# Attention scores on four row groups with four PSUM banks per unit, a new order of attention work, and weight preparation in pieces

## The chip, the core and the metric

The kernel runs on one core of a Trainium2 chip. The metric is device time in microseconds (us) of one execution. PE is the matrix engine, ACT the scalar engine (it does the exponentials), DVE the vector engine, POOL the GpSimd engine, SP the engine that issues most transfers. All engines work from static instruction lists, which are filled by a small list scheduler in the kernel's own source. It gives each operation an estimated duration and a priority (a lower number goes first), and fixes the order on every engine before anything runs. An edit to a priority, a bank or an engine therefore makes a new plan for all engines.

Times of one kernel mostly agree within 1%. Some runs are "slow" (over 1.5% above the fastest of the same kernel) and are kept out of comparisons. The ratios below are the mean time of one kernel's fast runs over that of the other's fast runs of the same rounds, so not quite the ratio of the medians that are quoted.

## The reference

A transformer block with two halves. The sequence has 2048 rows of width 448. The first half is attention with 16 heads of 28, in a sliding window of 256. The second is a gated MLP which also mixes along the sequence with a 2048 x 2048 matrix. Cut to what matters:

```python
h = layernorm(x) * (1 + ca) + sa
q, k, v = split(h @ wqkv)                        # 16 heads of 28
scores = einsum('bhqd,bhkd->bhqk', q, k) * 28**-0.5
p = softmax(where(0 <= q_idx - k_idx < 256, scores, -1e9))
x = x + ga * (einsum('bhqk,bhkd->bhqd', p, v) @ wo)
h = layernorm(x) * (1 + cb) + sb
z1, z2 = split(gelu(h @ w_in)); z2 = layernorm(z2)
x = x + gb * ((z1 * (w_sp @ z2 + b_sp)) @ w_out)
```

## The kernel before

The queries are worked in 16 blocks of 128 rows (`j`). Each block needs the scores against at most three key blocks (`kb`). Q and K are stored transposed and padded to 32 rows a head, four heads on top of each other, so a score matmul has a contraction of 32 and uses one of the array's four row groups. A score unit is 8 matmuls on two row groups, written to a pair of PSUM banks; one exp instruction on ACT then reads the whole pair.

```python
B_S = bank((0, 1), (2, 3))            # pairs for scores
B_MISC = bank((4,), (5,), (6,), (7,)) # PV, wo, projections, bias rows, gates
...
for hx in range(2):                              # half of the heads
    for bi, kb in enumerate(kbs):
        pr = j + (hx * nb + bi) / (2.0 * nb)     # priority of the unit
        ten = Ten(B_S)
        def s_fn(e, ...):
            for g in range(4):
                for i in range(2):
                    r = 2 * hx + i               # row group
                    last = mm(e, ps[:, ten.slot + i, g * 128:(g + 1) * 128],
                              QKT[32*r:32*r+32, 4+g, kb*128:(kb+1)*128],
                              QKT[32*r:32*r+32, g, j*128:(j+1)*128], True, True, tile_position=(32*r, 0))
        # exp on ACT, causal / window mask on POOL
    # PV of this half of the heads, priority j + 0.5 + 0.5 * hx + 0.1
# reciprocal and normalisation (DVE), transpose (DMA), wo (PE), residual x1, layernorm 2
```

The layernorm of the input (`xn`) runs on DVE. The second half's weights are prepared during attention: four bias rows (PE and a DVE cast), four products on `w_in`, and one product over all of `w_out` (`woutg`), which reads a gate from PSUM.

The softmax here doesn't subtract the row's maximum and nothing guards it: scores larger than these inputs give would overflow.

## Time and profile before

| | before |
|---|---|
| median of three runs | 331.76 us |
| first exp to last exp | 22.4 to 154.8 us |
| first MLP matmul to the end | 154.3 to 329.3 us: 175.1 us |
| TensorE clock at half speed after 20 us | 47.8 us |

The first lines to look at are the page's busy times and its rows of 40 slices (8.2 us a slice; a digit is tenths of the slice; PEclk is the granted TensorE clock).

```profile
PE 306.5 (93%) x2675; PEld 159.9 (49%) x2686; DVE 182.3 (55%) x405; ACT 131.9 (40%) x164; POOL 94.1 (29%) x110
...
PE   6697899799979999799999999999999999999995
...
ACT  3277167694666768898355666200000000000000
...
PEclk9789699999975589965899999999999999999999
```

There are two stages. From slice 19 on PE is full, from slice 20 on at full clock; that is the MLP. Before it PE has gaps, and besides short dips up to slice 4 the clock row has two long valleys, slices 11 to 14 and 17 to 19.

The first valley by stretches of 5 us. The columns are each engine's busy us with its number of instructions (PE, PEld, DVE, ACT, POOL), the mean granted clock, DMA share and GB/s.

```profile
90.00:95.00 5.00, 3.06 (x60) 2.19 (x60) 2.60 (x6) 2.86 (x4) 4.62 (x3) 0.91 0.64 124
95.00:100.00 5.00, 5.00 (x64) 3.05 (x60) 3.56 (x9) 3.86 (x4) 2.72 (x3) 0.50 0.16 37
100.00:105.00 5.00, 5.00 (x58) 2.70 (x54) 0.76 (x2) 3.07 (x3) 2.85 (x3) 0.50 0.49 88
105.00:110.00 5.00, 5.00 (x67) 3.09 (x66) 3.71 (x9) 3.49 (x4) 2.77 (x4) 0.50 0.32 66
110.00:115.00 5.00, 5.00 (x56) 2.46 (x55) 0.42 (x1) 3.50 (x4) 2.55 (x3) 0.50 0.45 89
```

PE idles for some 2 us of 90 to 95, and then the clock is half for 24 us. In those 24 us PE works more slowly: the `wo` matmuls start every 373 ns, against 189 at full clock, and the projections of 256 columns every 213, against 109 (medians of this trace).

The groups of instructions by shape (busy us, mean ns of one, then the idle time of the engine just before them and what ended it):

```profile
L625 ACT ACTIVATE PT<-ps 128x1024 bf16<-128x1024 f32 x90 | 88.1, 1026 | 39.5 <-PE ps L412 39.4
L412 PE MATMUL ps<-QKT 32*128 32x128 bf16 x720 | 38.2, 241 | 6.4 <-ACT PT L625 6.4
L490 DVE TENSOR_SCALAR xn<-x_sb,mv_all,rs_all 128x448 bf16<-128x448 bf16 x16 | 8.2, 545 | 1.0 <-POOL rs_all L465 0.9
```

ACT idles 39.5 us before its exps, and PE ended that idling. So PE is what holds attention up. A PE mean of 241 ns here is a latency, not a cost, because matmuls overlap: the eight of the unit below end 0.40 us after the first starts. The cost is read from the timeline as start to next start: the 8 matmuls of a unit, then the next kind.

```profile
122.19 0.40 PE L412 MATMUL ps<-QKT 32*128 32x128 bf16 x8
122.51 0.72 PE L412 MATMUL ps<-hT,WQK 112*128 112x256 bf16 x5
```

From 122.19 to 122.51 is the unit's cost. Over all warm units it is 0.328 us in the median, and 0.54 us at half clock.

### The profile page before, as it was taken

To read this page: it belongs to the slowest core of one execution; us is meant where nothing else is said; L and a number is where in the kernel's file an instruction comes from. 1 tells how busy PE (TensorE), PEld (TensorE's weight loads), DVE (VectorE), ACT (ScalarE), POOL (GpSimd) and SP (SyncE) were. 2 spreads that over 40 slices of the span, in tenths; PEclk is the share of its full clock that TensorE was granted. 3 is DMA by queue.
4 is the path that set the end of the run, shared out by engine and by line. 5 is a ranking of instruction groups with operands and counts; after the bars stand their busy time and mean duration, and the time that the engine had idled before them with its cause. 6 is when DMAs were issued, how large, how long until landed. Compare 5 with 4: busy or idle time off the path is not lost.

```text
span 329.3 us, 6418 instructions
## 1 busy us (share of the span) xinstructions
PE 306.5 (93%) x2675; PEld 159.9 (49%) x2686; DVE 182.3 (55%) x405; ACT 131.9 (40%) x164; POOL 94.1 (29%) x110
## 2 busy tenths in 40 slices
PE   6697899799979999799999999999999999999995
PEld 2464355364556466564444444444444444444442
DVE  5579898898853377644588772132243242324232
ACT  3277167694666768898355666200000000000000
POOL 4025336484474556776123121000000000000000
PEclk9789699999975589965899999999999999999999
DMA  7933794712335317575779900000010010001001
GB/s 188 275 105 66 156 192 126 192 36 50 65 66 99 66 34 114 90 114 115 147 133 218 180 2 0 0 2 0 0 58 0 0 39 19 0 2 56 0 0 56
DMA packets 67195, 25.18 MB, mean 76 GB/s; under 512 B 58464, under 2 KB 66592, under 8 KB 67168
## 3 DMA queue, kind: packets, MB, share of 16 engines
q1 hardware_dynamic: 67040, 24.79, 35.8%
q8 instruction: 21, 0.34, 0.5%
q14 instruction: 6, 0.05, 0.1%
q10 hardware_dynamic: 128, 0.00, 0.0%
HBM read 8.78 MB, written 1.84 MB: 32 GB/s over the span
## 4 chain that ended last, share of the span: by engine, by line
PE 79%; DVE 9%; DMA 5%; ACT 3%; issue 1%; POOL 1%; SPq 1%; DVEq 0%
PE ps L412 79%; ACT PT L625 3%; DMA x_sb<-in_A_x_dram 3%; DVE hT L529 3%; DVE xn L490 2%; DVE st_all L469 1%; DMA hT<-xn 1%; DMA oT<-o_sb 1%; DVE QKT L566 1%; POOL PT L633 1%; DVE wo_sb L458 1%; DVE hT L518 1%; DVE fin L839 0%; SPq L358 0%; DVE o_sb L657 0%
## 5 line engine op out<-in xcount | busy, mean ns | idle before, releaser
L625 ACT ACTIVATE PT<-ps 128x1024 bf16<-128x1024 f32 x90 | 88.1, 1026 | 39.5 <-PE ps L412 39.4
L633 POOL TENSOR_SCALAR_AFFINE_SELECT PT<-PT 128x1024 bf16<-128x1024 bf16 x60 | 68.8, 1157 | 39.8 <-ACT PT L625 39.5
L412 PE MATMUL ps<-w_spA,z 128*128 128x512 bf16 x327 | 76.3, 379 | 0.5
L817 DVE TENSOR_TENSOR tmpg<-ps,bsp_bc 128x512 bf16<-128x512 f32 x28 | 19.4, 692 | 74.5 <-PE ps L412 74.5
L412 PEld LDWEIGHTS ps<-w_spA,z 128*128 128x128 bf16 x336 | 32.9, 98 | 39.4
L412 PE MATMUL ps<-QKT 32*128 32x128 bf16 x720 | 38.2, 241 | 6.4 <-ACT PT L625 6.4
L412 PE MATMUL ps<-hT,WQK 112*128 112x256 bf16 (+1 forms) x192 | 42.4, 357 | 1.9 <-DVE hT L529 1.6
L465 POOL TENSOR_TENSOR rs_all<-ve_all,neghalf 128x1 f32<-128x1 f32 (+2 forms) x39 | 23.0, 597 | 65.2 <-DVE ve_all L463 65.0
L412 PEld LDWEIGHTS ps<-QKT 32*128 32x128 bf16 x720 | 23.0, 102 | 25.7 <-PE ps L412 19.9
L412 PE MATMUL ps<-w_spB,z 128*128 128x512 bf16 x110 | 28.5, 379 | 0.1
L412 PE MATMUL ps<-w_in_sb,hT 112*128 112x448 bf16 (+1 forms) x128 | 28.4, 366 | 0.0
L412 PE MATMUL ps<-hT,w_in_sb 112*128 112x512 bf16 x112 | 27.7, 387 | 0.0
L673 DVE TENSOR_TENSOR x_sb<-ps,x_sb 128x448 bf16<-128x448 f32 x16 | 9.9, 622 | 28.2 <-PE ps L412 28.2
L412 PEld LDWEIGHTS ps<-hT,WQK 112*128 112x128 bf16 x192 | 18.3, 109 | 14.9 <-DVE hT L529 3.6
L412 PEld LDWEIGHTS ps<-Vaug,PT 128*128 128x128 bf16 x720 | 22.1, 99 | 6.9 <-DVE QKT L566 1.8
L412 PE MATMUL ps<-Vaug,PT 128*128 128x29 bf16 x720 | 23.5, 179 | 1.3 <-POOL PT L633 1.3
L796 ACT ACTIVATE z1T<-ps 128x512 bf16<-128x512 f32 x28 | 16.7, 597 | 17.9 <-PE ps L412 17.9
L412 PE MATMUL ps<-w_out_sb,z1T 128*128 128x448 bf16 x112 | 21.8, 352 | 0.0
L566 DVE CAST QKT<-ps 128x256 bf16<-128x256 f32 (+1 forms) x33 | 17.7, 544 | 7.0 <-PE ps L412 6.7
L469 DVE BATCH_NORM_STATS2 st_all<-z2raw 128x6 f32<-128x448 bf16 x32 | 18.4, 607 | 3.4 <-ACT z2raw L776 3.4
L412 PE MATMUL ps<-wo_sb,oT 112*128 112x448 bf16 x64 | 18.1, 413 | 2.4 <-DVE QKT L566 2.0
L469 DVE BATCH_NORM_STATS2 st_all<-x_sb 128x6 f32<-128x448 bf16 x32 | 19.1, 606 | 1.8 <-DMA x_sb<-in_A_x_dram 1.5
(57 smaller groups left out, 239.9 us busy)
## 6 DMA issues: line engine op xcount, KB each, us to landing
out_dram<-fin SPq DMA_DIRECT2D x16, 112.0 KB, 1.7
wmod_sb<-in_w_mod_dram SPq DMA_DIRECT2D x2, 784.0 KB, 6.5
w_in_sb<-in_B_w_in_dram SPq DMA_DIRECT2D x4, 392.0 KB, 4.2
x_sb<-in_A_x_dram SPq DMA_DIRECT2D x3, 448.0 KB, 10.1
wqk_raw<-in_A_wqkv_dram SPq DMA_DIRECT2D x2, 392.0 KB, 8.3
wmod_sb<-in_w_mod_dram SPq DMA_DIRECT2D x2, 392.0 KB, 7.7
bsp_bc<-in_B_b_sp_dram SPq DMA_DIRECT2D x1, 512.0 KB, 4.6
x_sb<-in_A_x_dram SPq DMA_DIRECT2D x2, 224.0 KB, 5.9
```

The source lines that it names most:

```text
L412: return e.matmul(out_, lhsT=lhsT, rhs=rhs, start=st, stop=sp, **kw)
L458: t_wog = P.op("wog1", -1.1, [("dve", dve_ns(4 * D), lambda e: e.tensor_tensor(wo_sb[0:KP, :, :], wo_sb[0:KP, :, :], ps[0:KP, ten_g1.slot, ...
L465: return P.op(name + "rs", prio, [("pool", 515 + 150 * (t1 - t0 - 1), lambda e: e.tensor_tensor(rs_all[:, slot, t0:t1], ve_all[:, slot, t0 ...
L469: st = [P.op("%sst%d" % (name, i), prio, [("dve", dve_ns(D, base=65), lambda e, i=i, s_=s_: e.bn_stats(st_all[:, slot, t, i, :], s_()))], ...
L490: xn_op[t] = P.op("xn%d" % t, pr + 0.1, [("dve", 310, lambda e, t=t, ten=ten: e.tensor_scalar(xn[:, ten.slot, :, 0:KP], x_sb[:, t, :].rear ...
L529: hT_op[b].append(P.op("hT%d_%d" % (b, cc), pr + 0.1, [("dve", 190 + 0.27 * 128 * n, lambda e, cc=cc: e.tensor_scalar(hT[0:KP, cc, t0 * 12 ...
L566: return e.tensor_copy(QKT[:, g, t0 * 128:t1 * 128], ps[:, ten.slot, 0:n])
L625: return e.activation(PT[:, pt.slot, :, :], ps[:, ten.slot:ten.slot + 2, :], ACT.Exp, scale=SCALE)
L633: return e.affine_select(out=v, in_=v, pattern=[[0, 8], [s_, 128]], compare_op=ALU.is_ge if diag else ALU.is_gt, fill=0.0, base=0, channel ...
L673: x1_op[j] = P.op("x1_%d" % j, pr, [("dve", 545, lambda e, j=j, wt=wt: e.tensor_tensor(x_sb[:, j, :], ps[:, wt.slot, 0:D], x_sb[:, j, :], ...
L796: z1_op[(ft, tb)] = P.op("z1g%d_%d" % (tb, ft), pr, [("act", act_ns(512), lambda e, tb=tb, ft=ft, ten=ten: e.activation(z1T[:, ft, tb * 51 ...
L817: a = P.op("ga%d_%d" % (tb, ft), pr, [("dve", 610, lambda e, tb=tb, ten=ten, tg=tg: e.tensor_tensor(tmpg[:, tg.slot, :], ps[:, ten.slot, : ...
```

## The change

Its intent: use all four row groups at once, so that one unit of 16 matmuls does what two units of 8 did, in about the time of one. A unit then writes two bank pairs. To let the next unit start while ACT still reads the last one, there is a third pair, which leaves two single banks for everything else. The weight preparation is cut into pieces and moved to the end of attention. The diff also changes the order of work: scores get a priority four query blocks ahead (`j - 4`) and PV nearly three ahead (`j - 2.95`). Twelve of the sixteen `xn` go to POOL. Cut to its core:

```diff
-    B_S = bank((0, 1), (2, 3))
-    B_MISC = bank((4,), (5,), (6,), (7,))
+    B_S = bank((0, 1), (2, 3), (4, 5))
+    B_MISC = bank((6,), (7,))
@@
-        for hx in range(2):
-            for bi, kb in enumerate(kbs):
-                pr = j + (hx * nb + bi) / (2.0 * nb)
-                ten = Ten(B_S)
+        for bi, kb in enumerate(kbs):
+            pr = j - 4 + bi / float(nb)
+            tens = [Ten(B_S), Ten(B_S)]
@@
-                        for i in range(2):
-                            r = 2 * hx + i
-                            last = mm(e, ps[:, ten.slot + i, ...
+                    for r in range(4):
+                        last = mm(e, ps[:, tens[r // 2].slot + r % 2, ...
@@
-            pv = P.op("PV%d_%d" % (j, hx), j + 0.5 + 0.5 * hx + 0.1, ...
+            pv = P.op("PV%d_%d" % (j, hx), j - 2.95 + 0.01 * hx, ...
@@
-                xn_op[t] = P.op(..., [("dve", 310, ...
+                xn_op[t] = P.op(..., [("dve", 310, xn_fn)] if b < NPE else [("pool", 600, xn_fn)], ...
@@  bias rows from priority 6.3 to 10.5 and later, w_in products from 7.5 to 12.5 and later,
@@  both also held back to set score units (33 and on, 40 and on, of 45)
-    t_woutg = P.op("woutg", 9.3, one product over 7 x 448 from PSUM)
+    t_gb = P.op("gbcp", 13.3, copy of the gate to SBUF)
+    t_woutg = [P.op("woutg%d" % k, 150 + k, product over 448) for k in range(7)]
```

Cut away: the scheduler's support for an operation that takes two tensors of banks, the scaling of `wo` in four pieces, projections of the first blocks allowed in all banks, and new points in the list of score units from which later projections and weight loads may start.

More of the change, by code (lines that the diff above doesn't have):

```diff
@@ L66, in op @@
         self.ops.append(o)
-        if alloc is not None:
-            alloc(o)
+        for t in flat(alloc):
+            t(o)
         for t in flat(uses):
@@ L71, in op, with slot_time @@
         return o
-    def slot_time(self, ten):
+    def slot_time(self, ten, taken=()):
         best = None
@@ L77, in slot_time @@
             for r in opt:
+                if r in taken:
+                    tm = None
+                    break
                 prev = self.last.get(r)
@@ L105, in schedule @@
                 if o.alloc is not None:
-                    st = self.slot_time(o.alloc)
-                    if st is None:
+                    st, taken = [], []
+                    for ten in flat(o.alloc):
+                        got = self.slot_time(ten, taken)
+                        if got is None:
+                            break
+                        st.append((ten, got[1]))
+                        taken += got[1]
+                        dep_t = max(dep_t, got[0])
+                    if len(st) < len(list(flat(o.alloc))):
                         continue
-                    dep_t = max(dep_t, st[0])
                 best = None
@@ L126, in schedule @@
             if o.alloc is not None:
-                for r in st[1]:
-                    prev = self.last.get(r)
-                    if prev is not None:
-                        o.extra.extend(prev.users)
-                    self.last[r] = o.alloc
-                o.alloc.got = st[1]
+                for ten, slots in st:
+                    for r in slots:
+                        prev = self.last.get(r)
+                        if prev is not None:
+                            o.extra.extend(prev.users)
+                        self.last[r] = ten
+                    ten.got = slots
             o.eng, o.fn, o.start, o.end = eng, fn, est, fin
@@ L211, in run @@
                 fn(e).then_inc(self.sems[key], inc)
+REL = {2: (1, 8), 3: (8, 19), 4: (19, 28), 5: (28, 37)}
+MISC = (12, 33, 2, 40, 1, 33, 18, 4)
 def mm_ns(n):
@@ L251, in bass_adaLN_cond__sliding_block__mixer_gmlp__prompt_kernel @@
     SCALE = float(DH) ** -0.5
-    ARENA = 207 * 1024
+    ARENA = 207 * 1024 + 512
     arena = nc.alloc_sbuf_tensor("arena", [128, ARENA // 2], BF16)
@@ L285, in bass_adaLN_cond__sliding_block__mixer_gmlp__prompt_kernel @@
     neghalf, _, _ = alloc("neghalf", [128, NT], F32)
+    gb_sb, _, _ = alloc("gb_sb", [128, D], F32)
     w_spA, wspA_off, wspA_end = alloc("w_spA", [128, 12, S], BF16)
@@ L457, in bass_adaLN_cond__sliding_block__mixer_gmlp__prompt_kernel @@
     g1, ten_g1 = gate("gateA", -1.2, 2, t_wmG)
-    t_wog = P.op("wog1", -1.1, [("dve", dve_ns(4 * D), lambda e: e.tensor_tensor(
-        wo_sb[0:KP, :, :], wo_sb[0:KP, :, :], ps[0:KP, ten_g1.slot, 0:D].unsqueeze(1).broadcast_to([KP, KC, D]), ALU.mult))],
-        [g1, t_wo], uses=[ten_g1])
+    t_wog = [P.op("wog%d" % k, -1.1, [("dve", dve_ns(D), lambda e, k=k: e.tensor_tensor(
+        wo_sb[0:KP, k, :], wo_sb[0:KP, k, :], ps[0:KP, ten_g1.slot, 0:D], ALU.mult))], [g1, t_wo], uses=[ten_g1]) for k in range(KC)]
     def ln_rs(name, prio, slot, t0, t1, deps):
@@ L489, in ln1, with xn_fn @@
                 xn_ten[t] = ten
-                xn_op[t] = P.op("xn%d" % t, pr + 0.1, [("dve", 310, lambda e, t=t, ten=ten: e.tensor_scalar(
-                    xn[:, ten.slot, :, 0:KP], x_sb[:, t, :].rearrange("p (k d) -> p k d", d=KP), mv_all[:, 0, t, 0:1], rs_all[:, 0, t:t + 1],
-                    ALU.subtract, ALU.mult))], [rs, t_xpad], alloc=ten)
+                def xn_fn(e, t=t, ten=ten):
+                    return e.tensor_scalar(xn[:, ten.slot, :, 0:KP], x_sb[:, t, :].rearrange("p (k d) -> p k d", d=KP),
+                                           mv_all[:, 0, t, 0:1], rs_all[:, 0, t:t + 1], ALU.subtract, ALU.mult)
+                xn_op[t] = P.op("xn%d" % t, pr + 0.1, [("dve", 310, xn_fn)] if b < NPE else [("pool", 600, xn_fn)], [rs, t_xpad], alloc=ten)
     hT_op, xnT = {}, {}
@@ L502, in transp @@
             for cc in range(KC):
-                ten = Ten(B_MISC)
+                ten = Ten(B_ALL)
                 mms = []
@@ L528, in transp, with md_fn @@
             for cc in range(KC):
-                hT_op[b].append(P.op("hT%d_%d" % (b, cc), pr + 0.1, [("dve", 190 + 0.27 * 128 * n, lambda e, cc=cc: e.tensor_scalar(
-                    hT[0:KP, cc, t0 * 128:t1 * 128], hT[0:KP, cc, t0 * 128:t1 * 128],
-                    modT[0:KP, 4 + cc:5 + cc], modT[0:KP, cc:cc + 1], ALU.mult, ALU.add))], xnT[b] + t_modA))
+                def md_fn(e, cc=cc):
+                    return e.tensor_scalar(hT[0:KP, cc, t0 * 128:t1 * 128], hT[0:KP, cc, t0 * 128:t1 * 128],
+                                           modT[0:KP, 4 + cc:5 + cc], modT[0:KP, cc:cc + 1], ALU.mult, ALU.add)
+                hT_op[b].append(P.op("hT%d_%d" % (b, cc), pr + 0.1, [("dve", 190 + 0.27 * 128 * n, md_fn)], xnT[b] + t_modA))
     t_wqkc = []
@@ L550, in qkv @@
         for k, g in enumerate((0, 4, 1, 5, 2, 6, 3, 7)):
-            ten = Ten(B_MISC)
+            ten = Ten(B_ALL if b < 2 else B_MISC)
             m = []
@@ L571, in qkv @@
         for t in range(t0, t1):
-            ten = Ten(B_MISC)
+            ten = Ten(B_ALL if b < 2 else B_MISC)
             m = []
@@ L603, in bass_adaLN_cond__sliding_block__mixer_gmlp__prompt_kernel, with s_fn @@
         pvs = []
-        for hx in range(2):
-            halves = []
-            for bi, kb in enumerate(kbs):
-                pr = j + (hx * nb + bi) / (2.0 * nb)
-                ten = Ten(B_S)
-                def s_fn(e, j=j, kb=kb, hx=hx, ten=ten):
-                    last = None
-                    for g in range(4):
-                        for i in range(2):
-                            r = 2 * hx + i
-                            last = mm(e, ps[:, ten.slot + i, g * 128:(g + 1) * 128],
-                                      QKT[32 * r:32 * r + 32, 4 + g, kb * 128:(kb + 1) * 128],
-                                      QKT[32 * r:32 * r + 32, g, j * 128:(j + 1) * 128], True, True, tile_position=(32 * r, 0))
-                    return last
-                deps = [QK_op[(g, blk_of[j])] for g in range(4)] + [QK_op[(4 + g, blk_of[kb])] for g in range(4)]
-                s_op = P.op("S%d_%d_%d" % (j, hx, bi), pr, [("pe", 410, s_fn)], deps, alloc=ten)
-                all_S.append(s_op)
+        halves = {0: [], 1: []}
+        for bi, kb in enumerate(kbs):
+            pr = j - 4 + bi / float(nb)
+            tens = [Ten(B_S), Ten(B_S)]
+            def s_fn(e, j=j, kb=kb, tens=tens):
+                last = None
+                for g in range(4):
+                    for r in range(4):
+                        last = mm(e, ps[:, tens[r // 2].slot + r % 2, g * 128:(g + 1) * 128],
+                                  QKT[32 * r:32 * r + 32, 4 + g, kb * 128:(kb + 1) * 128],
+                                  QKT[32 * r:32 * r + 32, g, j * 128:(j + 1) * 128], True, True, tile_position=(32 * r, 0))
+                return last
+            deps = [QK_op[(g, blk_of[j])] for g in range(4)] + [QK_op[(4 + g, blk_of[kb])] for g in range(4)]
+            s_op = P.op("S%d_%d" % (j, bi), pr, [("pe", 410, s_fn)], deps, alloc=tens)
+            all_S.append(s_op)
+            for hx in range(2):
+                ten = tens[hx]
                 pt = Ten(rot("pt", NPT))
@@ L635, in bass_adaLN_cond__sliding_block__mixer_gmlp__prompt_kernel, with pv_fn @@
                     done = P.op("M%d_%d_%d" % (j, hx, bi), pr, [("pool", pool_ns(1024), m_pool)], [e_op], uses=[pt])
-                halves.append((kb, pt, done))
-            def pv_fn(e, hx=hx, halves=halves, nb=nb, pv_ten=pv_ten):
+                halves[hx].append((kb, pt, done))
+        for hx in range(2):
+            def pv_fn(e, hx=hx, halves=halves[hx], nb=nb, pv_ten=pv_ten):
                 last = None
@@ L646, in pv_fn @@
                 return last
-            pv = P.op("PV%d_%d" % (j, hx), j + 0.5 + 0.5 * hx + 0.1, [("pe", 8 * nb * 25.5, pv_fn)],
-                      [d for _, _, d in halves] + [V_op[kb] for kb in kbs],
-                      alloc=pv_ten if hx == 0 else None, uses=[pt for _, pt, _ in halves] + ([pv_ten] if hx else []), order=pvs[:1])
+            pv = P.op("PV%d_%d" % (j, hx), j - 2.95 + 0.01 * hx, [("pe", 8 * nb * 25.5, pv_fn)],
+                      [d for _, _, d in halves[hx]] + [V_op[kb] for kb in kbs],
+                      alloc=pv_ten if hx == 0 else None, uses=[pt for _, pt, _ in halves[hx]] + ([pv_ten] if hx else []), order=pvs[:1])
             pvs.append(pv)
@@ L669, in wo_fn @@
                 return mm(e, ps[:, wt.slot, 0:D], oT[0:KP, oTt.slot, kc, :], wo_sb[0:KP, kc, :], kc == 0, kc == KC - 1)
-            wos.append(P.op("wo%d_%d" % (j, kc), pr, [("pe", mm_ns(D), wo_fn)], [t1, t_wog], alloc=None if kc else wt,
+            wos.append(P.op("wo%d_%d" % (j, kc), pr, [("pe", mm_ns(D), wo_fn)], [t1] + t_wog, alloc=None if kc else wt,
                             uses=[oTt] + ([wt] if kc else []), order=wos[-1:]))
@@ L689, in bass_adaLN_cond__sliding_block__mixer_gmlp__prompt_kernel @@
         first_S[j] = i
-        i += 2 * min(j + 1, 3)
+        i += min(j + 1, 3)
     def release(ops, s0, s1):
@@ L695, in release @@
             o.order.append(all_S[max(0, min(NS - 1, k))])
-    release(chains[2], 2, first_S[4] - 2)
-    release(chains[3], first_S[4] - 2, first_S[8] - 3)
-    release(chains[4], first_S[8] - 3, first_S[12] - 9)
-    release(chains[5], first_S[12] - 9, first_S[14] - 3)
+    for b_, (s0, s1) in REL.items():
+        release(chains[b_], s0, s1)
     m2, ten_m2 = mod_cols("modB", 6.0, (3, 4), t_wmB)
@@ L714, in fn @@
             return last
-        b = P.op("bz%d" % q, 6.3 + 0.3 * q, [("pe", 4 * mm_ns(D), fn)], [t_sbT] + t_win, alloc=ten)
+        b = P.op("bz%d" % q, 10.5 + 0.5 * q, [("pe", 4 * mm_ns(D), fn)], [t_sbT] + t_win, alloc=ten)
         bias_mm.append(b)
-        bias_ev.append(P.op("bze%d" % q, 6.4 + 0.3 * q, [("dve", dve_ns(D), lambda e, q=q, ten=ten: e.tensor_copy(
+        bias_ev.append(P.op("bze%d" % q, 10.6 + 0.5 * q, [("dve", dve_ns(D), lambda e, q=q, ten=ten: e.tensor_copy(
             bias_row[0:1, q * D:(q + 1) * D], ps[0:1, ten.slot, 0:D]))], [b] + t_wqkc, uses=[ten]))
-    t_brow = P.op("brow", 7.5, [("sp", 400, lambda e: e.dma_start(w_in_sb[KP:KP + 1, 3, :], bias_row[0:1, :]))], bias_ev,
+    t_brow = P.op("brow", 12.5, [("sp", 400, lambda e: e.dma_start(w_in_sb[KP:KP + 1, 3, :], bias_row[0:1, :]))], bias_ev,
                   table="load", dma=(3584, 2500, 165.0))
@@ L722, in bass_adaLN_cond__sliding_block__mixer_gmlp__prompt_kernel @@
     for kc in range(KC):
-        t_wing.append(P.op("wing%d" % kc, 7.5 + kc * 0.5, [("dve", 670, lambda e, kc=kc: e.tensor_scalar(
+        t_wing.append(P.op("wing%d" % kc, 12.5 + kc * 0.5, [("dve", 670, lambda e, kc=kc: e.tensor_scalar(
             w_in_sb[0:KP, kc, :], w_in_sb[0:KP, kc, :], modT[0:KP, 12 + kc:13 + kc], None, ALU.mult))], bias_mm + t_modB))
-    g2, ten_g2 = gate("gateB", 9.2, 5, t_wmB)
-    t_woutg = P.op("woutg", 9.3, [("dve", dve_ns(7 * D), lambda e: e.tensor_tensor(
-        w_out_sb[:], w_out_sb[:], ps[:, ten_g2.slot, 0:D].unsqueeze(1).broadcast_to([128, 7, D]), ALU.mult))], [g2] + t_wout, uses=[ten_g2])
+    g2, ten_g2 = gate("gateB", 13.2, 5, t_wmB)
+    t_gb = P.op("gbcp", 13.3, [("dve", dve_ns(D), lambda e: e.tensor_copy(gb_sb[:], ps[:, ten_g2.slot, 0:D]))], [g2], uses=[ten_g2])
+    t_woutg = [P.op("woutg%d" % k, 150 + k, [("dve", dve_ns(D), lambda e, k=k: e.tensor_tensor(
+        w_out_sb[:, k, :], w_out_sb[:, k, :], gb_sb[:], ALU.mult))], [t_gb] + t_wout) for k in range(7)]
     for n, o in enumerate(t_wmB + t_win + t_wout):
         o.order.append(xnT[2][-1])
-        o.order.append(all_S[min(NS - 1, 6 + 2 * n)])
-    m2.order.append(all_S[first_S[5]])
+        o.order.append(all_S[min(NS - 1, 3 + n)])
+    m2.order.append(all_S[MISC[0]])
+    for q in range(4):
+        bias_mm[q].order.append(all_S[MISC[1] + MISC[2] * q])
+        t_wing[1 + q].order.append(all_S[MISC[3] + MISC[4] * q])
+    g2.order.append(all_S[MISC[5]])
     mod_done = [m1, m2, g1, g2]
@@ L749, in bass_adaLN_cond__sliding_block__mixer_gmlp__prompt_kernel @@
             if hf == 0:
-                o.order.append(all_S[min(NS - 1, first_S[7] + 4 * n)])
+                o.order.append(all_S[min(NS - 1, MISC[6] + MISC[7] * n // 2)])
             else:
@@ L835, in bass_adaLN_cond__sliding_block__mixer_gmlp__prompt_kernel @@
                 parts.append(P.op("out%d_%d" % (t, lo), pr + i * 0.01 + (0.1 if lo else 0), [("pe", (hi - lo) * mm_ns(D), fn)],
-                                  [u_op[(ft, tb)] for ft in range(lo, hi)] + [t_woutg], alloc=ten if lo == 0 else None,
+                                  [u_op[(ft, tb)] for ft in range(lo, hi)] + t_woutg, alloc=ten if lo == 0 else None,
                                   uses=[ten] if lo else [], order=parts[:1]))
```

## The prediction

> **What bounds it now.** The page gives PE 93% busy, DVE 55%, ACT 40%. By stretches of the trace there are two stages. From about 154 us to the end (329) PE is gap-free at clock 1.0: the gated-MLP stage, some 175 us, which the change hardly touches (seven short `w_out` products on a DVE with slack there). Before it lies attention, 20 to 154 us: 134 us, in which the timeline's start-to-start times give PE 122 us of issue and 12 us of idle. The 90 exps on ACT (1.03 us each, about 0.93 in a row) need only some 84 us, but run from 22 to 154: 1.47 us each. So PE, not ACT, paces attention, with DVE close behind between 25 and 80 us (18 of 20 us busy).
>
> **Cost of scores.** A score unit of 8 matmuls (two row groups) takes 0.33 us of PE warm: pairs step every 56 ns, 0.22 us, plus about 0.10 us before the next kind's weights load. At clock 0.5 it is 0.54 us. The 90 units cost 34 us.[...]
>
> **Removed.** 45 units of 16 matmuls on four row groups remain. If quartets step every 56 ns, a unit still takes 0.33 us; if each weight load needs its 25 to 28 ns (the spacing of the PV matmuls), 0.50. I expect 0.38: about 13 us of PE saved[...].
> Twelve `xn` (0.55 us on DVE) go to POOL. The four of the first big block end at 28 us, held up by the 2.0 us `wo` product; on POOL they would end near 23. The exps' gap of 33 to 43 us, which waits for that block, shrinks: 4 us.
> The 3.4 us `w_out` product and the bias preparation leave mid-attention.
>
> **Added.** Score pairs take six PSUM banks; PV, `wo`, projections and bias share two instead of four. By my estimate per query block: PV holds a bank 3.3 us (less than now: both halves come together), `wo` 2, three projections 2 each: 11 us on two banks, 5.5 us, about ACT's 5.7 for six exps. New PE waits for DVE evictions: +4 us.
>
> **Clock.** The page's clock row and the stretches show 0.5 from 94 to 118 and 142 to 159 us, each after a few us of PE idling. I estimate 15 us lost to it in attention (`wo` matmul 387 against 208 ns). A denser PE should lose less, but as ACT comes nearer to bounding, idling returns late in attention: −4 us.
>
> **Sum.** −13 −4 −4 +4 = −17, and −1 for preparation moved into idle time: 331.8 − 18 = about 314 us, range 300 to 327. Chances: faster 0.82, same 0.13, slower 0.05.
>
> **What would show it.** The last exp at about 136 us instead of 154, 1.2 to 1.3 us per exp; the dense stage still 174 to 176 us; a warm 16-matmul unit at 0.33 to 0.50 us; PE waits on the QKT, Vaug and x_sb evictions up from about 5 us to 10; POOL `xn` of 0.6 to 0.9 us; half-clock time after 20 us down from 48 us to about 30.
>
> **What would make it wrong.** Two banks serialise PE with DVE so that PE idles some us at a time and the clock halves for most of attention (325 to 335). POOL `xn` at over 1 us[...]. Four row groups not running side by side. On the other side, if the clock stays at 1.0 and ACT alone paces (1.0 us per exp from 22 us), 297 to 302.

That quartets would step like the pairs in the trace, the bank times (the timeline from 60 to 75 us has `wo` hold a bank for 1.6 and 2.8 us) and the 0.6 to 0.9 us for an `xn` on POOL were my estimates.

## The result and the profile after

The changed kernel took 306.9 us in the median (305.75 to 307.69, four runs) against 333.07 for the kernel before in the same rounds (two of its four runs were slow; the two fast ones took 329.34 and 331.76). The ratio of the fast runs is 0.928, with an interval of 0.920 to 0.936. The result is correct.

The page's rows after (a slice is 7.6 us):

```profile
PE 281.1 (93%) x2675; PEld 143.8 (47%) x2686; DVE 176.8 (58%) x407; ACT 127.1 (42%) x160; POOL 113.2 (37%) x122
...
PE   6779698689998999899999999999999999999994
...
ACT  4267684497898987893556660000000000000000
POOL 5059999986876977842222200000000000000000
PEclk9998899799999999999999999999999999999998
```

The two valleys of the clock are gone; half clock after 20 us is down from 47.8 to 10.2 us (a last 1.8 us at the very end of the span, after the matmuls, left out). ACT is denser, and POOL is full from slice 3 to 7. The share of PE stayed at 93%, which shows how little that number says here.

The groups after:

```profile
L642 ACT ACTIVATE PT<-ps 128x1024 bf16<-128x1024 f32 x90 | 85.2, 1032 | 24.1 <-PE ps L428 23.9
L506 POOL TENSOR_SCALAR xn<-x_sb,mv_all,rs_all 128x448 bf16<-128x448 bf16 x12 | 22.5, 1879 | 0.1
L428 PE MATMUL ps<-QKT 32*128 32x128 bf16 x720 | 18.7, 222 | 0.4 <-ACT PT L642 0.2
```

The busy time of the score matmuls halved, and ACT idles 15 us less before its exps. An `xn` takes 1.88 us on POOL (twelve of twelve between 1.857 and 2.042), against 0.55 on DVE (means; the medians are 1.86 and 0.39, as three of the sixteen on DVE in the kernel before take over 1 us). A mask of 128x1024 takes 1.09 us on the same POOL.

A unit in the timeline after:

```profile
107.12 0.40 PE L428 MATMUL ps<-QKT 32*128 32x128 bf16 x16
107.46 0.93 PE L428 MATMUL ps<-wo_sb,oT 112*128 112x448 bf16 x4
```

Sixteen matmuls now cost what eight did: 0.335 us in the median of the warm units, against 0.328. Their single starts come in quartets 56 ns apart (100.732, 100.797, 100.853, 100.909), where before they came in pairs 56 ns apart. So matmuls of the four row groups run side by side here: the four of the first quartet start within 10 ns (100.732 to 100.742) and each is shown with some 224 ns. The kernel gives each row group a bank of its own; no run here tests another layout. Sixteen outputs of 128 columns fill four banks of 512 (the kernel's `ps` is 128 x 8 x 512) in any case.

The accounting that the rest rests on takes PE from 20 us to the first MLP matmul. Each start-to-next-start is put down to full clock or half clock, gaps apart. (The stretch that straddles 20 us is left out, so sums can fall some 1 us short.)

| PE in attention, us | at full clock | at half clock | idle | of this, scores | ends at | MLP to the end |
|---|---|---|---|---|---|---|
| before | 81.9 | 39.8 | 12.5 | 33.9 | 154.3 | 175.1 |
| after | 86.9 | 9.9 | 11.9 | 15.9 | 130.0 | 173.8 |

PE issue went from 121.7 to 96.8 us, idle hardly moved, and the MLP lost 1.3 us. Scores fell by 18.0 us. The other 7 us are the same instructions, by and large at a better clock (in order_and_prep below, which has 1.2 us of half clock, they take as little as after: 80 us). So far this looks like the prediction's story. The experiments showed that it is not all of it.

### The profile page after: what moved, and what is told of

It is laid out like the page before. It is cut to its first block, busy times and chain, and to the rows that moved or that the text cites. A ratio compares the mean times of both kernels' runs of the same rounds, so it can differ in the third digit from the quotient of the medians.

```text
span 303.8 us, 6429 instructions
## 1 busy us (share of the span) xinstructions
PE 281.1 (93%) x2675; PEld 143.8 (47%) x2686; DVE 176.8 (58%) x407; ACT 127.1 (42%) x160; POOL 113.2 (37%) x122
## 4 chain that ended last, share of the span: by engine, by line
PE 67%; DVE 11%; POOL 11%; DMA 5%; issue 3%; SPq 1%; DVEq 0%
PE ps L428 67%; POOL xn L506 6%; POOL PT L650 4%; DMA x_sb<-in_A_x_dram 3%; DMA oT<-o_sb 2%; DVE st_all L484 2%; DVE x_sb L690 2%; POOL rs_all L480 2%; DVE w_in_sb L738 1%; DVE xn L695 1%; DVE o_sb L674 1%; DVE QKT L583 1%; DVE w_out_sb L742 1%; SPq L374 1%; DVE hT L546 1%
## 5 line engine op out<-in xcount | busy, mean ns | idle before, releaser
L642 ACT ACTIVATE PT<-ps 128x1024 bf16<-128x1024 f32 x90 | 85.2, 1032 | 24.1 <-PE ps L428 23.9
L650 POOL TENSOR_SCALAR_AFFINE_SELECT PT<-PT 128x1024 bf16<-128x1024 bf16 x60 | 65.3, 1118 | 14.4 <-ACT PT L642 14.4
L428 PE MATMUL ps<-hT,WQK 112*128 112x256 bf16 (+1 forms) x192 | 35.4, 319 | 4.6 <-ACT hT L530 1.6
L428 PE MATMUL ps<-w_in_sb,hT 112*128 112x448 bf16 (+1 forms) x128 | 26.8, 352 | 0.0
L428 PEld LDWEIGHTS ps<-Vaug,PT 128*128 128x128 bf16 x720 | 20.2, 96 | 8.8 <-PE ps L428 5.3
L506 POOL TENSOR_SCALAR xn<-x_sb,mv_all,rs_all 128x448 bf16<-128x448 bf16 x12 | 22.5, 1879 | 0.1
L796 ACT ACTIVATE z2raw<-ps 128x896 bf16<-128x896 f32 x16 | 14.6, 917 | 15.5 <-DVE z L801 9.5
L428 PE MATMUL ps<-QKT 32*128 32x128 bf16 x720 | 18.7, 222 | 0.4 <-ACT PT L642 0.2
L428 PE MATMUL ps<-wv_sb,hT 112*128 112x448 bf16 x64 | 15.9, 378 | 3.3 <-DVE QKT L583 3.2
L428 PEld LDWEIGHTS ps<-w_in_sb,hT 112*128 112x128 bf16 (+1 forms) x128 | 12.4, 97 | 12.7
## 6 DMA issues: line engine op xcount, KB each, us to landing
out_dram<-fin SPq DMA_DIRECT2D x16, 112.0 KB, 1.7
```

The costliest lines, as they stand in the source:

```text
L428: return e.matmul(out_, lhsT=lhsT, rhs=rhs, start=st, stop=sp, **kw)
L506: return e.tensor_scalar(xn[:, ten.slot, :, 0:KP], x_sb[:, t, :].rearrange("p (k d) -> p k d", d=KP), mv_all[:, 0, t, 0:1], rs_all[:, 0, t ...
L642: return e.activation(PT[:, pt.slot, :, :], ps[:, ten.slot:ten.slot + 2, :], ACT.Exp, scale=SCALE)
L650: return e.affine_select(out=v, in_=v, pattern=[[0, 8], [s_, 128]], compare_op=ALU.is_ge if diag else ALU.is_gt, fill=0.0, base=0, channel ...
L796: g = P.op("z2g%d" % t, pr, [("act", act_ns(FH), lambda e, ten=ten, zt=zt: e.activation(z2raw[:, zt.slot, :].rearrange("p (a d) -> p a d", ...
```

## The experiments

Twelve kernels ran; all gave correct results. "Ratio" is against the kernel before of the same rounds. None of the intervals below contains 1; that of halves lies within 2% of it. No plan was searched for the kernels that undo a part, except in replanned: each result is that of its edit together with the plan that the scheduler made of it.

| run | median us | ratio | 95% interval |
|---|---|---|---|
| the change | 306.90 | 0.928 | 0.920 to 0.936 |
| pairs_in_turn | 307.85 | 0.928 | 0.919 to 0.937 |
| xn_dve | 303.95 | 0.917 | 0.908 to 0.927 |
| scores_alone | 317.84 | 0.957 | 0.947 to 0.966 |
| two_pairs | 341.32 | 1.032 | 1.021 to 1.042 |
| scores_twice | 317.05 | 0.951 | 0.946 to 0.957 |
| halves | 335.19 | 1.008 | 1.002 to 1.014 |
| lookahead_alone | 314.72 | 0.947 | 0.941 to 0.952 |
| wout_late | 315.64 | 0.950 | 0.943 to 0.957 |
| merged_old_order | 316.88 | 0.958 | 0.955 to 0.961 |
| order_and_prep | 310.48 | 0.938 | 0.934 to 0.943 |
| lookahead_banks | 342.53 | 1.037 | 1.030 to 1.044 |
| replanned | 305.94 | 0.926 | 0.922 to 0.930 |

My theory was that PE time saved by concurrent row groups is the main part of the gain. The rivals: that it is the order of work, the banks, the moved preparation, or the clock.

### pairs_in_turn: row groups 0 and 1 first, then 2 and 3

```diff
-                for g in range(4):
-                    for r in range(4):
+                for r0 in (0, 2):
+                  for g in range(4):
+                    for r in (r0, r0 + 1):
```

> The changed kernel, each score unit's 16 matmuls reordered: row groups 0 and 1 for all four head groups, then 2 and 3. Banks, plan, xn on POOL and all else as in the changed kernel. Theory (concurrent row groups save PE time): pairs step every 56 ns again, a warm unit takes about 0.57 instead of 0.35 us, 45 units cost some 10 us more PE; as ACT also waits longer for its first half-pair, the total rises by 6 to 10 us, to 313 to 317. Rival A (the gain is the order of work and the banks, not concurrency): within 2 us of the changed kernel. Rival B (the gain is the clock that a denser PE keeps): PE is even denser here, so the clock stays at 1.0 and the time within 3 us.

Measured: 307.85 us, 1 us over the changed kernel. This looks like rival A, but the experiment did not do what I wanted. A warm unit took 0.355 us and not 0.57: the sixteen starts lie within about 0.21 us, and the third row group starts 0.12 us after the first. Row groups overlapped although they were not neighbours in the list, so this order takes away hardly any concurrency. The run refutes my estimate of 0.57 us and tells nothing of the rivals.

### scores_twice: give the saved PE time back, keep the plan

```diff
-                for g in range(4):
+                for g in (0, 1, 2, 3, 0, 1, 2, 3):
```

> The changed kernel with every score matmul issued twice into the same place (same result): the plan, banks and order stay, a warm unit takes about 0.335 + 0.224 = 0.56 us instead of 0.335, so 45 units cost 10 us more of PE; that gives back two thirds of the PE time that the merged units save (90 x 0.328 - 45 x 0.335 = 14.4 us). Theory (PE time saved by concurrency is a main part of the gain): 313 to 318. Rival (PE has slack in attention and the gain is order, banks and clock): at most 3 us over the changed kernel, 307 to 310.

Measured: 317.05 us, 10 us over the changed kernel (8 by the ratios), in the theory's range. The plan, the banks and the order are those of the changed kernel to the instruction; only PE works longer. Its profiled run was slow, so its trace is not used. About 10 us of PE time cost 8 to 10 us of total time: in this kernel PE time in attention counts nearly in full. This is the clean support for one half of the theory, that PE time counts here. That the time saved by merging is the main part of the gain it does not show.

### xn_dve: all xn back on DVE

```diff
-[("dve", 310, xn_fn)] if b < NPE else [("pool", 600, xn_fn)]
+[("dve", 310, xn_fn)]
```

> The changed kernel with all sixteen xn on DVE as before. Each xn took 1.88 us on POOL against 0.55 on DVE, and POOL is busy without a gap from 20 to 62 us. Theory (POOL is what paces 20 to 62 us): the last exp of query block 4 moves from 59 us to about 53, total 4 to 7 us faster, 299 to 302. Rival (DVE, already 90% busy there, takes over as the limit): within 2 us of the changed kernel or slower.

Measured: 303.95 us, 3 us under the changed kernel; 3.6 by the ratios, whose intervals overlap in part. That is the theory's direction, but between its range and the rival's "within 2 us". It is the fastest kernel. In the changed kernel's timeline POOL looks like this:

```profile
19.45 1.87 POOL L506 TENSOR_SCALAR xn<-x_sb,mv_all,rs_all 128x448 bf16<-128x448 bf16 x1
21.28 2.15 POOL L650 TENSOR_SCALAR_AFFINE_SELECT PT<-PT 128x1024 bf16<-128x1024 bf16 x2
23.42 5.55 POOL L506 TENSOR_SCALAR xn<-x_sb,mv_all,rs_all 128x448 bf16<-128x448 bf16 x3
28.93 2.14 POOL L650 TENSOR_SCALAR_AFFINE_SELECT PT<-PT 128x1024 bf16<-128x1024 bf16 x2
```

The list goes on without a gap to 62 us, and masks that PV waits for queue behind the `xn`. The four `xn` of the first big block end at 29 us, no earlier than on DVE before (28). With `xn` on DVE the last exp of block 4 starts at 55.1 us instead of 58.8.

### two_pairs: no third bank pair

```diff
-    B_S = bank((0, 1), (2, 3), (4, 5))
-    B_MISC = bank((6,), (7,))
+    B_S = bank((0, 1), (2, 3))
+    B_MISC = bank((4,), (5,), (6,), (7,))
```

> The changed kernel with only two bank pairs for scores, 0-1 and 2-3, and four single banks 4 to 7. A unit then waits for both exps of the one before, so ACT should idle some 0.6 us (semaphores and the first quartets) at each of 45 units: Theory (the third pair matters): ACT idle before the exps up from 24 us by 15 to 25, total 8 to 20 us slower, 315 to 327. Rival (two single banks are what is scarce): faster than the changed kernel, under 305.

Measured: 341.32 us, 34 us over the changed kernel and slower than the kernel before. The direction was right; the size was over the upper end. ACT idles 57 us before its exps, as in this piece of its timeline:

```profile
112.96 1.94 ACT L642 ACTIVATE PT<-ps 128x1024 bf16<-128x1024 f32 x2 [0.71 <-PE ps L428]
115.49 1.94 ACT L642 ACTIVATE PT<-ps 128x1024 bf16<-128x1024 f32 x2 [0.60 <-PE ps L428]
118.03 1.94 ACT L642 ACTIVATE PT<-ps 128x1024 bf16<-128x1024 f32 x2 [0.60 <-PE ps L428]
```

After each two exps ACT waits 0.6 us or more for the next unit, because PE may not write it before both pairs are read. Of the 0.60 us before the exp at 110.31, 0.14 lie between the end of the two exps (109.72) and the unit's first matmul (109.86), and 0.45 between that and the exp. PE waits in its turn (40 us idle in attention), and the clock is half for 51 us (the profiled run was the slowest of the four, 344.81 us). So the third pair is not a detail of the merged units: with the plan that the scheduler makes without it, the whole gain is lost.

### lookahead_alone: only the order, on the kernel before

```diff
-                pr = j + (hx * nb + bi) / (2.0 * nb)
+                pr = j - 4 + (hx * nb + bi) / (2.0 * nb)
-            pv = P.op("PV%d_%d" % (j, hx), j + 0.5 + 0.5 * hx + 0.1, ...
+            pv = P.op("PV%d_%d" % (j, hx), j - 2.95 + 0.01 * hx, ...
```

> The kernel before with one thing alone: scores planned four query blocks ahead and PV three ahead, so that the exps are fed first. Rival of the row groups: it is this order that brings the gain, then 305 to 315. Theory: PE stays the limit at its old cost, so 325 to 333.

Measured: 314.72 us, 18 us faster than the kernel before, with no row groups merged, no bank moved and no `xn` on POOL. It lands inside the rival's range. The page's rows:

```profile
PE   6799979999998999989999999999999999999994
...
PEclk9989999999999589989999999999999999999999
```

One narrow dip of the clock is left of the two valleys. The instructions on PE are the same as before, but in attention their issue fell from 121.7 to 111.1 us and PE's idle time from 12.5 to 6.1. With scores and PV put before the projections and the preparation, PE is less often left without work.

### halves: the changed kernel with units of 8 again

```diff
-                    for r in range(4):
+                    for r in (2 * hx, 2 * hx + 1):
@@ one operation for each hx, with one bank pair each, in place of one with two pairs
```

> The changed kernel with each score unit split again into two of 8 matmuls on two row groups and one bank pair, in the same order of blocks, with three pairs, two single banks, the score-first priorities, the late preparation and xn on POOL. A unit should take 0.33 us again, so 90 of them cost 14 us more PE than 45 merged ones. Theory (merging matters): 314 to 322. Rival (all but the merging brings the gain): 304 to 310.

Measured: 335.19 us, 28 us over the changed kernel and 20 over lookahead_alone. It is far over both ranges. PE issues 123.0 us in attention, of which 38.1 at half clock. The extra PE cost (14 us) does not explain 28; the rest is that half clock and 4 us more idle. Here the same score-first order runs with three pairs and two single banks. The exps come in long bursts and then wait: ACT idles 13.9 us in block 4, 9.2 in block 8 and 8.9 in block 14, mostly before a block's first exp, while PE works off the next projections.

### lookahead_banks: three pairs and two single banks alone

```diff
-    B_S = bank((0, 1), (2, 3))
-    B_MISC = bank((4,), (5,), (6,), (7,))
+    B_S = bank((0, 1), (2, 3), (4, 5))
+    B_MISC = bank((6,), (7,))
```

This is an edit to lookahead_alone.

> lookahead_alone (314.7 us) with one edit: three bank pairs for the units of 8 and two single banks, instead of two pairs and four. Theory C (two single banks are a cost, which the merged units need the third pair to bear: halves, with the same banks, took 335): 325 to 340, with PE waiting for DVE evictions. Rival (the third pair is what helps; halves was slow for the POOL xn or its plan): 308 to 316.

Measured: 342.53 us, 28 us over lookahead_alone: for units of 8 the new split of banks is a loss. The longest waits of this kernel (us in total, times, longest):

```profile
ACT PT L625 <- PE ps L412: 53.3, 11, 19.7
...
DVE x_sb L673 <- PE ps L412: 14.9, 12, 3.5
...
PE ps L412 <- DVE x_sb L673: 7.1, 6, 4.8
```

ACT's idle time is in eleven waits, up to 19.7 us: the exps have run ahead and wait for a whole block of projections, which now pass through two banks. I had expected PE to wait for evictions, and this is in part so (7.1 us for `x_sb`); the larger loss is 50.2 us of issue at half clock (in the profiled run, at 346.48 us the slowest; its granted clock was 0.90, that of the other three 0.92).

### merged_old_order: the changed kernel with the old order

```diff
-            pr = j - 4 + bi / float(nb)
+            pr = j + bi / float(nb)
-            pv = P.op("PV%d_%d" % (j, hx), j - 2.95 + 0.01 * hx, ...
+            pv = P.op("PV%d_%d" % (j, hx), j + 0.5 + 0.5 * hx + 0.1, ...
```

> The changed kernel with the old priorities alone: a query block's scores at its own turn instead of four blocks ahead, its PV after them instead of three blocks ahead. Theory C (order and merging are two gains: order removes PE idling and the half clock, 18 us as lookahead_alone showed; merging removes PE work): 315 to 325, with more PE idle and more than 20 us of half clock. Rival (with merged units PE has room enough, and order no longer matters): 305 to 311.

Measured: 316.88 us: 10 us over the changed kernel, 14 under the kernel before, with 19.0 us of PE idle and 22.4 us of half clock between the first exp and the MLP (13.7 and 10.2 in the changed kernel). The theory of two gains holds.

### order_and_prep: new order and late preparation, units of 8, old banks

The edit is lookahead_alone with the changed kernel's seven `w_out` products and its later bias rows, `w_in` products and gate.

> The kernel before (units of 8, two bank pairs, four single banks, xn on DVE) with the new order and the late weight preparation, in pieces. Theory C (what is left to the merged units and their banks is the difference to xn_dve, which took 304): 311 to 316, so merging is worth 7 to 12 us on top. Rival (order and late preparation are the whole gain): 302 to 307.

Measured: 310.48 us, half a us under the theory's range and above the rival's. Against lookahead_alone the late preparation gives 4 us by the medians and 3 by the ratios, whose intervals touch. Against xn_dve, 6.5 us are left for the merged units and their banks. PE has next to no losses here: 108.0 us at full clock, 1.2 at half clock, 5.0 idle.

The last two runs complete a table (medians in us):

| | units of 8 on two row groups | units of 16 on four |
|---|---|---|
| old order | 331.8 (before) | 316.9 (merged_old_order) |
| new order | 310.5 (order_and_prep) | 306.9 (the change), 304.0 (xn_dve) |

The columns also differ in the banks, and the upper left has the early preparation, so this is not a pure two by two. It shows the shape: the two gains overlap. Order and late preparation take away PE's idle time and half clock at unchanged work. Merging takes away work, 29.0 us of scores in order_and_prep down to 15.9, but then PE idles 12 us instead of 5, and part of the gain goes there. So the step from left to right is worth some 14 us in the old order (with the late preparation in it) and 4 to 7 in the new one.

### scores_alone and wout_late: early preparation with the merged units

scores_alone is xn_dve with the bias rows, the `w_in` products and the seven `w_out` products at early priorities, released from score unit 12 on. wout_late leaves `w_out` at the changed kernel's priority.

```diff
-MISC = (12, 33, 2, 40, 1, 33, 18, 4)
+MISC = (12, 12, 0, 12, 0, 12, 18, 4)
-    P.op("woutg%d" % k, 150 + k, ...        # scores_alone only
+    P.op("woutg%d" % k, 9.3 + 0.01 * k, ...
```

> Score units of 16 on four row groups with the new banks and order, xn on DVE, and the second half's weight preparation at its old time (from query block 4 to 6). Theory (the score units carry nearly all of the gain): 302 to 308. Rival (moving the preparation out of the middle carries 5 us or more): over 308, with PE waits on evictions between 70 and 95 us.

> As scores_alone (xn on DVE, bias and w_in products early), but with the seven w_out products left to the MLP stage. Theory (in scores_alone these seven, 6.9 us in a row on DVE, held the two single banks, and PE idled 6.4 us and the clock halved for 14 us): back to 303 to 308. Rival (the bias rows and w_in products early cost as much): 311 to 318.

Measured: 317.84 and 315.64 us, 14 and 12 us over xn_dve. The rival was right that early preparation is costly: nearly three times the 5 us I had named, and wout_late lies in its rival's range. The waits came later than I had said, though: in scores_alone ACT's exps stop from 106 to 119 us. Two lines of its timeline in that stretch: DVE holds a row of six `w_out` products, and PE waits for a normalisation (`o_sb`) that queues behind them:

```profile
102.41 6.92 DVE L742 TENSOR_TENSOR w_out_sb<-w_out_sb,gb_sb 128x448 bf16<-128x448 bf16 x6
...
110.76 1.46 PE L428 MATMUL ps<-Vaug,PT 128*128 128x29 bf16 x48 [6.44 <-DVE o_sb L674]
```

With two single banks, one of them waiting for that normalisation, PE has nowhere to write. wout_late was to show that these products are the cause, and failed to: its gate was still early, and the scheduler put a low-priority product wherever DVE was idle, so they ran at 101 to 110 us anyway, among the normalisations. Its exps stop in the same place, for 10.7 us. What is shown is that early preparation as a whole costs 12 to 14 us with two single banks, and 4 us with four (lookahead_alone against order_and_prep). How it divides between bias rows, `w_in` and `w_out` stays open.

### replanned: measured durations in the scheduler, and a new search

The edit is xn_dve with the scheduler's costs set to measured ones, then release points and priorities searched for the shortest plan. The search gave up the `j - 4` and `j - 2.95`:

```diff
-            pr = j - 4 + bi / float(nb)
+            pr = j - 0 + bi / float(nb)
-            pv = P.op("PV%d_%d" % (j, hx), j - 2.95 + 0.01 * hx, ...
+            pv = P.op("PV%d_%d" % (j, hx), j - 0.5 + 0.01 * hx, ...
```

> xn_dve with the costs that the list scheduler plans with set to measured durations (cast of 512: 0.68, score unit 0.335, x1 and normalisation 0.62, mod of a block 0.69 us and so on), and the release points and priorities searched again under them. If the plan made with wrong costs is what still idles ACT (22 us before the exps in xn_dve): 294 to 301. If the rest is limits that no plan removes: 301 to 306.

Measured: 305.94 us, no better than xn_dve (ratios 0.926 and 0.917). Its exps took less time, 107.3 us from first to last against 112.0, but started 4 us later (22.4 against 18.4 us). So the second expectation stands: with this structure, nothing near 297 us came out of planning. It also shows that the gain of order does not hang on these two numbers: other priorities, with release points to match, do about as well.

## Why the prediction was right or wrong

The time: 314 (300 to 327) was predicted and 306.9 measured; direction and range were right. The gain is 24 us, fast runs against fast runs (26 by the medians, which for the kernel before include two slow runs), against the 18 predicted. Step by step:

- "PE, not ACT, paces attention": right. ACT's idle time ended with PE in both traces, and scores_twice turns about 10 us of PE time into 8 to 10 us of total time.
- "about 13 us of PE saved" by the units: nearly right. The quartets step every 56 ns as the hopeful case had it, a warm unit costs 0.335 us and not 0.38, and at full clock that saves 90 x 0.328 - 45 x 0.335 = 14.4 us. Scores fell by 18.0 us (33.9 to 15.9), which includes the better clock.
- "on POOL they would end near 23 ... 4 us": failed. An `xn` takes 1.86 us on POOL, not 0.6 to 0.9, an estimate that no trace backed. They end at 29 us, and POOL is full to 62 us. Undoing this part makes the kernel some 3 us faster, at the edge of the noise.
- "New PE waits for DVE evictions: +4 us": not seen as such. PE's idle time in attention is 11.9 us against 12.5, and its waits for the QKT eviction are 3.2 us against 2.7. The scarcity of two banks is real, but shows where something is added: 28 us for units of 8 in the new order (lookahead_banks), 12 to 14 us for early preparation.
- "Clock ... −4 us": the main miss. Issue at half clock fell from 39.8 to 9.9 us where I had expected half-clock time to fall to 30 of 48. By an estimate from the sums above the clock gave some 10 us (7 on other instructions, 18.0 - 14.4 on scores), not 4. "As ACT comes nearer to bounding, idling returns late in attention" did not happen.
- "and −1 for preparation moved": far too small. With four single banks it is 3 to 4 us; with two, 12 to 14.
- What the sum left out altogether is the order of work. The priorities `j - 4` and `j - 2.95` were in the diff, and I gave them no term. Alone they gain 18 us on the kernel before. They bring down the idle time and half clock (47.8 to 13.7 us in lookahead_alone) that I had expected a denser PE to bring down by itself. That the total still fell in the range is in part luck: the missing gain was larger than the losses I had mis-sized.
- "1.2 to 1.3 us per exp": right, 113.8 us for 90. "The last exp at about 136": it ended at 131.9. "The dense stage still 174 to 176": 173.8 us, just under.

What went with the clock can be read from two traces, the kernel before and the changed one, by a count that was made only after the experiments. In their clock records the stretches of half clock that ended before the last matmul lasted 3.413, 6.827, 17.067 and 23.893 us, which are 1, 2, 5 and 7 times 3.413. Cut each trace into pieces of 3.413 us, with the clock's changes at their ends, and for each piece add up the matmuls that start in it, each as its columns times rows/128: a score matmul of 128 columns on 32 rows counts 32. The 21 pieces that half clock followed (17 before the change, 4 after) had at most 3056; the 162 that full clock followed (79 and 83) had at least 3256, whether the clock in the piece itself was half or full.

In the kernel before the piece from 90.7 us had 2520. The next six, at half clock and with PE shown busy throughout, had 2432 to 3056, and the clock stayed. The seventh had 3304, and the clock returned. A unit of 8 comes to 256 in 0.328 us warm and in 0.54 us at half clock, one of 16 to 512 in 0.335 us: merging raises this count as well as saving time. This is what two traces show; a count over all 14 traces had two of 1270 pieces on the wrong side with the starts as they are recorded. Why the clock changes is not shown, and no run was made to test the count.

What stays open is how much of the order's gain comes from scores and how much from PV, and what a plan searched for the other splits of banks would give.

## What to carry to other kernels

Take every priority in a static plan as a change of its own and cost it: putting attention before the other work (18 us alone) was worth as much as merging its score units (14 us, late preparation included), and the two gains overlap. When a unit takes more banks at once, count how many units must be in flight; one pair short here turned a gain of 24 us into a loss of 10 (fast runs). Do not read the clock from the busy share: here it was half for 24 us with PE shown busy throughout, while columns times rows of the matmuls per 3.413 us told the pieces apart in both traces. Before an elementwise operation moves to an engine that is idle on average, find a duration of the same operation on that engine in a trace: 1.86 us in place of 0.39 filled an engine that had looked free.
